# Two float32 layers behind a retention block: Strassen-like products against three-pass products of float32r parts, in two phases

## The chip, the core and the metric

The kernel runs on one core of a Trainium2 chip. The core has five engines with queues of their own: TensorE (PE in the profile, its weight loads PEld), VectorE (DVE), ScalarE (ACT), GpSimd (POOL) and SyncE (SP), which here only issues DMAs. They share an on-chip memory of 128 partitions, and TensorE writes its sums to eight PSUM banks of 512 float32 values per partition. The metric is the device time of one execution in microseconds; a version's time is the median of its runs.

## The reference

A retention block (a linear attention with a decaying state) over batch 4, 8 heads, 768 steps, head width 64, then two dense layers with an activation between them, over 4 x 768 = 3072 tokens:

```python
for t in range(S):
    state = gamma * state + np.einsum('bhd,bhe->bhde', k[:, :, t], v[:, :, t])
    y[:, :, t] = scale * np.einsum('bhd,bhde->bhe', q[:, :, t], state)
...
x = attn_out.transpose(0, 2, 1, 3).reshape(B * S, H * D)      # 3072 x 512
h = x @ w_in                                                   # w_in 512 x 2048
sp = np.maximum(h, 0.0) + np.log1p(np.exp(-np.abs(h)))         # softplus
g = h * erf(sp)
return (g @ w_out).astype(np.float32)                          # w_out 2048 x 512
```

q, k, v and the result are float32; w_in and w_out come as float64.

## The kernel before

The retention block works in 24 chunks of 128 steps. Chunks 0 to 3 take a longer way (`ret_scale`, `ret_transpose` on TensorE, `ret_scores`, `ret_mask`, `ret_out`). From chunk 4 on a chunk is handled as two halves of 64 steps: scores and state additions (`sub_begin`, or inside `sub_visit`), mask and new states on VectorE, results on TensorE, copies on ScalarE and two small sums on VectorE. Keys and queries from chunk 6 on are not transposed by TensorE: `load_blocks` fetches them in 32 x 32 blocks with 16 small DMAs for each of k and q (L187), and `prepared` scales them and transposes the blocks on VectorE. What comes out is x transposed (`xT`), the moving operand of the first layer.

The weights come as 64-bit words. `conversion` makes float32 of one piece (256 rows or columns, 1 MB) with five VectorE instructions and one of ScalarE. Its steps are handed out by `need` (until a block of weights is there) and `pace` (a budget of steps per matmul work). From the sixth piece on (in the changed kernel from the fifth to the seventh), `weights` puts the first step of the next piece between the third and fourth step of the present one.

The first 512 tokens go through both layers in plain float32 matmuls: `hidden_of` (L860) for the first layer, 512 columns at a time, `project` (L896) for the second. The rest runs in chunks of 256 tokens, each in two halves of the hidden width, so 20 groups `g`. Both layers then use bilinear schemes with fewer products: `hidden_steps` (L951) makes 26 products of blocks where 32 would be plain, from 18 sums of x (`X_SUMS`) and precomputed sums of the weights (`W_SUMS`), and adds or subtracts the products from PSUM into eight result blocks, on VectorE (L963) or ScalarE (L965, L967); `project_part` (L1034) makes 7 products where 8 would be plain, from sums of the gated values (`g_sums`) and of w_out. Between them `gate_softplus` (L817) and `gate_erf` (L830) on ScalarE and `gated` (L849) on VectorE. One group of the first layer runs in turn with products of the second layer of the group before it, so TensorE has work of one while VectorE and ScalarE finish the other. The first of these groups uses `hidden_plain` (L980) while sums of weights are still being made.

The order on every engine is the order in which the code is written (a manual schedule). All DMAs but two small ones and those for sums of w_out are issued by SP, in order; `load_block_scales` (L469, L473), with 17 tiny loads, stands at the third group. Outputs leave with `put_first` and `put_part`.

Of the kernel before, what the change touches and what calls it, by code (L numbers as in the profile page):

```python
# [12 lines left out]
F32 = mybir.dt.float32  # L13
U32 = mybir.dt.uint32
I64 = mybir.dt.int64
# [6 lines left out]
TCH = 512  # L22
FG = 4
SCH = 256
CV = 2


# [4 lines left out]

OUT = {"11": 0, "12": 1, "21": 2, "22": 3, "T3": 1, "T1": 4, "T2": 5, "T4": 6}

PRODUCTS = {
    1: ("11", "11"), 2: ("12", "21"), 3: ("S4", "22"), 4: ("22", "T4"),
    5: ("S1", "T1"), 6: ("S2", "T2"), 7: ("S3", "T3"),
}
# [6 lines left out]
N_W, N_X = 26, 18  # L45
W_SUMS = (
    (16, 2, 6, "+"),
    (17, 8, 10, "-"),
    (4, 4, 17, "+"),
    (10, 10, 16, "+"),  # L50
    (18, 16, 4, "-"),
    (19, 18, 5, "-"),
    (20, 1, 19, "-"),
    (20, 0, 20, "+"),
    (21, 9, 20, "+"),
    (9, 13, 9, "-"),
    (22, 15, 13, "-"),
    (23, 15, 9, "-"),
    (7, 3, 7, "+"),
    (24, 20, 12, "-"),  # L60
    (25, 18, 7, "+"),
    (2, 2, 3, "+"),
    (8, 12, 8, "-"),
    (12, 17, 12, "-"),
    (3, 3, 15, "-"),
    (15, 2, 15, "-"),
    (19, 19, 13, "-"),
    (16, 16, 7, "+"),
    (7, 7, 10, "+"),
    (4, 4, 6, "-"),  # L70
    (1, 1, 5, "+"),
    (5, 5, 2, "+"),
    (6, 14, 12, "+"),
    (6, 6, 15, "-"),
    (13, 23, 11, "-"),
    (13, 13, 7, "-"),
)

X_SUMS = (
    (0, (1, 0), (1, 1), "-"),  # L80
    (1, (0, 0), (0, 1), "-"),
    (2, (0, 0), (1, 0), "-"),
    (3, (1, 1), (0, 1), "-"),
    (4, (3, 0), (2, 0), "-"),
    (5, 1, 2, "-"),
    (6, (2, 0), 1, "+"),
    (7, (3, 1), 0, "-"),
    (8, (1, 1), (3, 1), "+"),
    (9, 6, (0, 1), "+"),
    (10, 7, 4, "-"),  # L90
    (11, (2, 0), 10, "-"),
    (12, (2, 1), 6, "-"),
    (13, (3, 1), 12, "-"),
    (14, 9, 13, "-"),
    (15, (3, 0), 13, "-"),
    (16, 15, 2, "+"),
    (17, 1, 15, "+"),
)

STEPS = (  # L100
    (21, (1, 0), 0, True, ((4, True),)),
    (20, 5, 1, True, ((1, False),)),
    (10, 14, 2, True, ((3, True),)),
    (22, 0, 3, True, ((5, True),)),
    (23, 7, 0, False, ((5, True),)),
    (24, (0, 1), 1, False, ((7, False),)),
    (25, 15, 2, False, ((2, True),)),
    (14, (2, 1), 3, False, ((7, True),)),
    (9, 8, 0, False, ((7, True),)),
    (12, 6, 1, False, ((6, False),)),  # L110
    (2, 11, 2, True, ((2, False), (6, True))),
    (17, 1, 3, True, ((2, False), (4, True))),
    (15, 10, 0, False, ((6, True),)),
    (8, 9, 1, False, ((4, False),)),
    (3, 4, 0, False, ()),
    (19, (1, 0), 0, False, ((0, True),)),
    (7, 13, 1, False, ((2, True),)),
    (0, 2, 2, False, ((0, True),)),
    (18, 16, 0, False, ((2, False),)),
    (16, 12, 1, False, ((3, True),)),  # L120
    (6, (2, 0), 3, False, ((6, True),)),
    (11, (3, 0), 2, True, ((4, True),)),
    (5, 0, 0, False, ()),
    (4, 17, 0, False, ((3, False),)),
    (1, 3, 0, False, ((1, True),)),
    (13, (3, 1), 1, False, ((5, False),)),
)

OP = {"+": ALU.add, "-": ALU.subtract}

BELOW = 1023 - 127
# [3 lines left out]
def kernel(  # L137
# [18 lines left out]
    NJ = B * NC  # L156
    n_k = d_model // P
    n_ft = d_ff // P
    JPC = TCH // C
    TT = TCH // P  # L160
    N = FG * TCH
    DH = d_model // 2
    assert D == 64 and d_model == H * D and n_k == HP == 4 and S % C == 0 and NJ % JPC == 0
    assert H == 8 and n_ft == 4 * FG and SCH == 2 * C and TCH == 2 * SCH

    const = ctx.enter_context(tc.tile_pool(name="const", bufs=1))
    loads = ctx.enter_context(tc.tile_pool(name="loads", bufs=3))
    ret = ctx.enter_context(tc.tile_pool(name="ret", bufs=2))
    act = ctx.enter_context(tc.tile_pool(name="act", bufs=2))
# [4 lines left out]


    early = True
    KQ, V, KB = {}, {}, {}

    NB = JPC + 2

    def load_blocks(to, src):


        for s, d in itertools.product(range(2), range(2)):
            part = slice((2 * s + d) * 32, (2 * s + d + 1) * 32)
            for u in range(HP):
                nc.sync.dma_start(  # L187
                    to[part, u * C : (u + 1) * C].rearrange("p (a d) -> p a d", d=32),
                    src[2 * u + s, :, d * 32 : (d + 1) * 32].rearrange("(a p) d -> p a d", p=32),
                )  # L190

    def load(j):
        b, c = divmod(j, NC)
        if j == JPC - 1:

            x = act.tile([P, N], F32, name="e", bufs=1)
            KQ[j] = x[:, : 2 * d_model].rearrange("p (i h d) -> p i h d", i=2, h=H)
            V[j] = x[:, 2 * d_model : 3 * d_model].rearrange("p (h d) -> p h d", h=H)
        else:
            KQ[j] = loads.tile([P, 2, H, D], F32, name="kq")  # L200
            V[j] = loads.tile([P, H, D], F32, name="v")
        now = slice(c * C, (c + 1) * C)
        if j >= NB:
            KB[j] = loads.tile([P, HP * C], F32, name="kb", bufs=2)
            nc.sync.dma_start(KQ[j][:, 0], k[b, :, now, :].rearrange("h p d -> p h d"))
            load_blocks(KQ[j][:, 1].rearrange("p h d -> p (h d)"), q[b, :, now, :])
            load_blocks(KB[j], k[b, :, now, :])
        for i, src in enumerate((k, q) if j < NB else ()):
            nc.sync.dma_start(KQ[j][:, i], src[b, :, now, :].rearrange("h p d -> p h d"))
        if not early:  # L210
            load_values(j)

    def load_values(j):
        b, c = divmod(j, NC)
        nc.sync.dma_start(V[j], v[b, :, c * C : (c + 1) * C, :].rearrange("h p d -> p h d"))
# [6 lines left out]
    w_in_sb = const.tile([P, 2, N_W, 2 * P], F32, name="w_in_sb")  # L222
    w_out_sb = const.tile([P, 2, 7, FG, DH], F32, name="w_out_sb")

    def w_in_of(ft, kk):
        half, s, i = ft // (2 * FG), ft % (2 * FG) // FG, ft % FG
        return w_in_sb[:, s, 4 * (2 * half + i // 2) + kk, i % 2 * P : (i % 2 + 1) * P]

    def w_out_of(ft):
        half, s, i = ft // (2 * FG), ft % (2 * FG) // FG, ft % FG  # L230
        return w_out_sb[:, s, 2 * half : 2 * half + 2, i, :]

    CE = 2 * d_model
    spare = [w_out_sb[:, s, 4:7].rearrange("p a b c -> p (a b c)") for s in range(2)]
    spare += [w_in_sb[:, s, 16:24].rearrange("p a f -> p (a f)") for s in (1, 0)]
    raws = [x[:, : 2 * CE].bitcast(I64) for x in spare]

    def halves(x):  # L240
        return x.rearrange("p (h c) -> p h c", h=2).bitcast(U32)

# [5 lines left out]
    for n in range(4):  # L248
        if n < 3:
            pieces += [("in", 2 * n + 2), ("in", 2 * n + 3)]  # L250
# [1099 lines left out]
```

## Time and profile before

| | us |
|---|---|
| runs (3), lowest / median / highest | 662.51 / 663.13 / 664.62 |
| span of the profiled execution | 660.9 |
| TensorE busy, weight loads busy | 655.7, 557.3 |
| VectorE, ScalarE, GpSimd busy | 508.4, 280.2, 11.7 |
| DMA | 51.88 MB, mean 78 GB/s |
| granted TensorE clock, mean | 1.000 |

The span runs from the first to the last instruction of the profiled execution. A row of the profile gives line, engine, operation, output and input tiles, shape and count, then the busy time and the mean of one in ns, then the idle time just before and what ended it. Matmuls are pipelined, so the mean of one is longer than the distance between two; the distance is read from the timeline, whose rows give start, length and a count of merged instructions. SPq rows are the DMA issues of SP's queue.

### The profile page before, as it was taken

Reading aid. Unit: us, or ns where it says so; the run is one execution under the profiler, and the core shown is the slowest. Engines: PE = TensorE matmul, PEld = TensorE weight load, DVE = VectorE, ACT = ScalarE, POOL = GpSimd, SP = SyncE. Lnnn points to the kernel's source line nnn. Section 1 sums busy time; section 2 is a strip of 40 time slices with the busy share of each in tenths; the row PEclk is TensorE's granted clock in tenths of the full one; section 3 lists DMA queues with packets and bytes.
Section 4 is the critical chain, followed back from the end, with each engine's and each line's share of the span. In section 5 each row is a group of like instructions: output and inputs, shape, how many; then the busy total and the mean of one; then the engine's idle time right before and its main releaser. Section 6 shows DMA issues by size and latency. Waiting matters only on the chain.

```text
span 660.9 us, 15247 instructions
## 1 busy us (share of the span) xinstructions
PE 655.7 (99%) x6200; PEld 557.3 (84%) x6200; DVE 508.4 (77%) x1102; ACT 280.2 (42%) x402; POOL 11.7 (2%) x29
## 2 busy tenths in 40 slices
PE   8999999999999999999999999999999999999998
PEld 7744444576999999999999999999999999999997
DVE  5999999969986786788678678677687688476464
ACT  3468363445534334244254253342432542533440
POOL 1000000110100000000000000000000000000000
PEclk9999999999999999999999999999999999999999
DMA  9999844385753321222222322221231210000000
GB/s 188 223 264 231 211 129 107 63 152 90 144 123 61 85 47 32 67 47 46 70 44 47 73 39 46 42 72 37 44 79 36 46 53 1 2 34 0 1 33 32
DMA packets 159413, 51.88 MB, mean 78 GB/s; under 512 B 143216, under 2 KB 149744, under 8 KB 159344
## 3 DMA queue, kind: packets, MB, share of 16 engines
q1 hardware_dynamic: 157776, 46.72, 32.8%
q0 software_dynamic: 1152, 4.19, 3.4%
q8 instruction: 48, 0.79, 0.5%
q14 instruction: 21, 0.17, 0.1%
q10 hardware_dynamic: 416, 0.01, 0.0%
HBM read 40.39 MB, written 6.29 MB: 71 GB/s over the span
## 4 chain that ended last, share of the span: by engine, by line
PE 98%; DMA 1%; DVE 0%; ACT 0%; issue 0%
PE o L1034 37%; PE hp L951 22%; PE r L951 12%; PE hp L860 8%; PE o L896 8%; PE hp L980 2%; PE r L736 2%; PE hp L628 1%; PE o L772 1%; PE r L524 1%; PE r L557 1%; PE o L604 1%; PE r L751 1%; PE hp L751 1%; DMA kq<-in_k_dram 1%; PE r L772 0%
## 5 line engine op out<-in xcount | busy, mean ns | idle before, releaser
L1034 PE MATMUL o<-w_out_sb,h 128*128 128x256 f32 (+1 forms) x640 | 142.7, 380 | 0.0
L951 PE MATMUL hp<-xs,w_in_sb 128*128 128x128 f32 x988 | 138.1, 275 | 0.0
L1034 PEld LDWEIGHTS o<-w_out_sb,h 128*128 128x128 f32 x640 | 119.5, 190 | 16.6
L963 DVE TENSOR_TENSOR h<-h,hp 128x256 f32<-128x256 f32 x190 | 78.0, 418 | 70.5 <-PE hp L951 65.6
L951 PEld LDWEIGHTS hp<-xs,w_in_sb 128*128 128x128 f32 x988 | 128.4, 192 | 3.0
L1034 PE MATMUL o<-w_out_sb,e 128*128 128x256 f32 x480 | 113.5, 379 | 0.0
L1034 PEld LDWEIGHTS o<-w_out_sb,e 128*128 128x128 f32 x480 | 86.8, 190 | 9.4
L817 ACT ACTIVATE e<-h 128x2048 f32<-128x2048 f32 x22 | 42.1, 1912 | 119.6 <-DVE h L963 119.6
L963 DVE TENSOR_TENSOR h<-h,r 128x256 f32<-128x256 f32 x152 | 56.9, 415 | 22.3 <-PE r L951 21.4
L965 ACT COPY h<-hp 128x256 f32<-128x256 f32 x38 | 14.2, 373 | 130.7 <-PE hp L951 122.7
L951 PE MATMUL r<-xs,w_in_sb 128*128 128x128 f32 x456 | 63.3, 275 | 0.0
L951 PEld LDWEIGHTS r<-xs,w_in_sb 128*128 128x128 f32 x456 | 57.0, 192 | 0.0
L860 PE MATMUL hp<-xT,w_in_sb 128*128 128x512 f32 (+2 forms) x144 | 56.5, 548 | 0.0
L849 DVE TENSOR_TENSOR e<-h,e 128x1024 f32<-128x1024 f32 x42 | 49.2, 1213 | 8.0 <-ACT e L830 8.0
L860 PEld LDWEIGHTS hp<-xT,w_in_sb 128*128 128x128 f32 x144 | 25.8, 190 | 27.0 <-issue 24.6
L951 PE MATMUL hp<-xT,w_in_sb 128*128 128x128 f32 x304 | 46.3, 275 | 0.0
L951 PEld LDWEIGHTS hp<-xT,w_in_sb 128*128 128x128 f32 x304 | 41.5, 192 | 1.4 <-issue 0.5
L830 ACT ACTIVATE e<-e 128x2048 f32<-128x2048 f32 (+1 forms) x23 | 42.1, 1836 | 0.2
L967 ACT ACTIVATE h<-hp 128x256 f32<-128x256 f32 x57 | 21.9, 384 | 29.7 <-PE hp L951 28.3
L951 PE MATMUL r<-xT,w_in_sb 128*128 128x128 f32 x228 | 31.7, 275 | 0.0
L830 ACT ACT_TABLE_LOAD x24 | 30.8, 1283 | 0.4
L951 PEld LDWEIGHTS r<-xT,w_in_sb 128*128 128x128 f32 x228 | 28.5, 192 | 0.0
(164 smaller groups left out, 799.0 us busy)
## 6 DMA issues: line engine op xcount, KB each, us to landing
w_out_sb<-in_moe_w_out_dram SPq DMA_DIRECT2D x14, 512.0 KB, 5.2
kq<-in_k_dram SPq DMA_DIRECT2D x23, 256.0 KB, 4.0
v<-in_v_dram SPq DMA_DIRECT2D x23, 256.0 KB, 3.4
out_dram<-r SPq DMA_DIRECT2D x23, 256.0 KB, 2.9
kq<-in_q_dram SPq DMA_DIRECT2D x288, 16.0 KB, 1.9
kb<-in_k_dram SPq DMA_DIRECT2D x288, 16.0 KB, 1.8
w_in_sb<-in_moe_w_in_dram SPq DMA_DIRECT2D x8, 512.0 KB, 10.1
w_out_sb<-w_out_sb POOLq DMA_DIRECT2D x8, 512.0 KB, 5.3
```

The source lines that it names most:

```text
L736: nc.tensor.matmul(pp[r][col * D : (col + 1) * D, u % 2, t], x[own, u, :], QT[j][own, u, t], start=first(r, col), stop=True, skip_group_ch ...
L751: nc.tensor.matmul(other[a][own, u % 2, D:] if crossed else pp[a][own, u % 2, t], V[j][t, 2 * u + r, :], AM[j][t, r, u, :D], start=crossed ...
L817: nc.scalar.activation(E[g], HS[g], AF.Softplus)
L830: nc.scalar.activation(E[g][:, half], E[g][:, half], AF.Erf)
L849: nc.vector.tensor_tensor(E[g][:, half], HS[g][:, half], E[g][:, half], op=ALU.mult)
L860: nc.tensor.matmul(HP_[ft][:, t], w_in_of(ft, kk), XC[0][:, kk, t], start=(kk == 0), stop=(kk == n_k - 1),)
L896: nc.tensor.matmul(O[0][tt].rearrange("p (d c) -> p d c", d=2), E[g][:, u * TCH + tt * P : u * TCH + (tt + 1) * P], w_out_of(ft), start=(f ...
L951: nc.tensor.matmul(to[:, u, :], w_in_sb[:, s, w, u * P : (u + 1) * P], XS[m](x), start=first and u == 0, stop=True, skip_group_check=True,)
L963: nc.vector.tensor_tensor(h, h, of, op=ALU.add if plus else ALU.subtract)
L965: nc.scalar.copy(h, of)
L967: nc.scalar.activation(h, of, AF.Copy, scale=-1.0)
L1034: nc.tensor.matmul(O[m][i][:, half, at], G[g][a][:, u * P : (u + 1) * P], w_out_sb[:, s, OUT[b], u, at], start=i not in started, stop=(s = ...
```

## The change

The file is written anew in most of its parts. Retention for chunks 0 to 5, the conversion of weights and the start are kept in substance. These differ:

- Both layers become plain products without Strassen-like sums. Each float32 factor is split into parts that a float32r operand holds exactly: `hi` (rounded by ScalarE as it writes float32r), `lo` (the rest) and `dif` (a combination of both). Three matmuls in float32r, of `hi`, `lo` and `dif`, into two PSUM sums, and `together` (one ScalarE and one VectorE instruction) combine to the full product.
- Phase one does retention and the first layer for all 3072 tokens, in groups of 256, each in 8 units of 256 hidden rows (`unit`). The sums h are stored to DRAM tiles `HID`, 25 MB in all. Groups 0 and 1 (the first 512 tokens) use plain float32 matmuls (`hidden_of`, 256 columns each), with stores in `put_hidden`.
- Phase two reads h back by halves of a group (`load_hidden`, 1 MB), gates it (`gate`, `gated`), splits it (`split_g`) and multiplies by w_out (`project`), 48 steps of 24 matmuls with 512 columns.
- w_out is converted during phase one, stored as float32 in DRAM (`WOF`) and read back and split at the end of phase one; the split of w_in is made around group 2.
- Keys and queries are loaded and prepared for two chunks at once (`load_pair`, `prepare`): 32 small DMAs and 4 larger ones per pair, five VectorE instructions of twice the width.
- `load_block_scales` moves to the first 128 hidden rows of the first 512 tokens.

The core of the diff (what the new functions replace is the code described above):

```diff
+Z = 2.0**-12
+KEEP = 1.0 - 2.0**-13
...
+    def split_weights(n, w=None):
+        w = WF.pop(n) if w is None else w
+        hi, lo, dif = (b4(f"w_{x}", [2 * d_model], F32R) for x in ("hi", "lo", "dif"))
...
+        nc.scalar.activation(hi, w, AF.Copy, scale=KEEP * Z)
+        nc.vector.scalar_tensor_tensor(lo, hi.bitcast(F32), -1 / Z, w, op0=ALU.mult, op1=ALU.add)
+        nc.vector.tensor_tensor(dif, hi.bitcast(F32), lo.bitcast(F32), op=ALU.subtract)
+        W[n] = hi, lo, dif
+
+    def split(to, at, x):
+        hi, lo, dif = (t[at] for t in to)
+        nc.scalar.activation(hi, x, AF.Copy, scale=KEEP)
+        nc.vector.tensor_tensor(lo, x, hi.bitcast(F32), op=ALU.subtract)
+        nc.vector.scalar_tensor_tensor(
+            dif, hi.bitcast(F32), Z, lo.bitcast(F32), op0=ALU.mult, op1=ALU.subtract
+        )
+
+    def together(to, a, b):
+        nc.scalar.activation(to, a, AF.Copy, scale=1 + 1 / Z)
+        nc.vector.scalar_tensor_tensor(to, b, -1 / Z, to, op0=ALU.mult, op1=ALU.add)
...
+    def load_pair(j):
...
+            for to, src in ((KB[j], k), (QB[j], q)):
+                for u in range(HP):
+                    nc.sync.dma_start(
+                        to[part, u].rearrange("p (a d) -> p a d", d=32),
+                        src[b, 2 * u + s, c * C : (c + 2) * C, d * 32 : (d + 1) * 32].rearrange(
+                            "(a p) d -> p a d", p=32
+                        ),
+                    )
+                yield
...
+    def unit(g, n):
+        if n in W:
+            own = next(turn)
+            a, b = (ps_o.tile([P, 2, GT], F32, name=f"o{2 * own + i}") for i in range(2))
+            for to, parts in ((a, (0, 1)), (b, (2,))):
+                for u in range(2):
+                    for kk, i in itertools.product(range(n_k), parts):
+                        nc.tensor.matmul(
+                            to[:, u],
+                            W[n][i][:, kk * 2 * P + u * P : kk * 2 * P + (u + 1) * P],
+                            X[g][i][:, kk],
...
+        def put():
+            h = b2("h", [2, GT])
...
+                together(h, a, b)
+            nc.sync.dma_start(HID[g][:, 2 * n : 2 * n + 2], h)
+        return put
...
+    during = {
+        0: [(load_block_scales,)],
+        1: [(K_, a)],
+        2: [(T, a, None, ("o2", "o3")), (steps, pair, 2)],
...
+        14: [(split_weights, 0)],
+        15: [(split_weights, 1)],
+    }
+    for ft in range(n_ft):
+        need("in", ft)
+        if ft:
+            hidden_of(ft, 0)
+        hidden_of(ft, 1)
...
+        need("in", min(ft + 2, n_ft - 1))
+        for f, *args in during.get(ft, ()):
+            f(*args)
+        put_hidden(ft)
...
+    def project(n):
...
+        for f, t in order:
+            ft = 4 * i + f
+            a, b = Y[g][t]
+            for x, to in enumerate((a, a, b)):
+                nc.tensor.matmul(
+                    to,
+                    G[n][x][:, f, t * P : (t + 1) * P],
+                    W[ft // 2][x][:, ft % 2 * d_model : (ft % 2 + 1) * d_model],
...
+    to_out = {
+        0: [(load_hidden, 0), (load_w_out, 0), (gate, 0)],
+        1: [(gated, 0), (load_hidden, 1), (load_w_out, 1), (split_w_out, 0)],
+        2: [(split_g, 0), (load_w_out, 2), (split_w_out, 1)],
+        3: [(split_g, 1), (load_w_out, 3), (split_w_out, 2)],
+        4: [(gate, 1), (load_w_out, 4), (split_w_out, 3)],
+        5: [(gated, 1), (load_hidden, 2), (load_w_out, 5), (split_w_out, 4)],
+        6: [(load_w_out, 6), (split_w_out, 5)],
+        7: [(load_w_out, 7), (split_w_out, 6)],
+    }
+    for g in range(G2, NG):
+        a, b = 2 * g + 2, 2 * g + 3
...
+        for n in range(NPC):
+            if more:
+                for f, j in {0: [(begin, a)], 2: [(results, a)], 3: [(begin, b)], 5: [(results, b)]}.get(n, ()):
+                    f(j)
+            put = unit(g, n)
+            steps(pair, 2)
+            if g == G2 and n < 4:
+                split_weights(n + 2)
+            if g == G2 + 1 and n in (1, 4):
+                split_weights(6 + n // 4)
+            if more:
+                if n == 0:
+                    states(a)
...
+                steps(prep, {5: 1, 6: 1, 7: 3}.get(n, 0))
+            if g > G2:
+                convert({1: 2, 2: 1, 4: 2}.get(n, 0) if a + 2 < NJ else 1)
+            put()
+            if g == NG - 1:
+                W.pop(n)
+                for f, *args in to_out[n]:
+                    f(*args)
+    split_w_out(NPC - 1)
+    for n in range(NG * NU):
+        g, i = divmod(n, NU)
+        project(n)
+        if n % 2 == 0:
+            split_g(n + 2)
+            if i == 0 and g:
+                for t in range(2):
+                    put_out(g - 1, t)
+            split_g(n + 3)
+            gate(n // 2 + 2)
+        else:
+            gated(n // 2 + 2)
+            load_hidden(n // 2 + 3)
```

## The prediction

> **What bounds the kernel now.** I read the page's busy lines and the chain of waits first, then TensorE's timeline for the true spacing of matmuls (a row's mean is a latency, since matmuls overlap), then the rows of the other engines and the DMA queue for prices.
>
> ```profile
> span 660.9 us, 15247 instructions
> PE 655.7 (99%) x6200; PEld 557.3 (84%) x6200; DVE 508.4 (77%) x1102; ACT 280.2 (42%) x402; POOL 11.7 (2%) x29
> ...
> PE 98%; DMA 1%; DVE 0%; ACT 0%; issue 0%
> ```
>
> TensorE alone sets the end, at full granted clock, so the change is worth what it does to TensorE's stream, plus any gap it opens in it. The timeline (start, length, name, count):
>
> ```profile
> 54.45 14.00 PE L896 MATMUL o<-w_out_sb,e 128*128 128x512 f32 x32
> 68.29 10.46 PE L860 MATMUL hp<-xT,w_in_sb 128*128 128x512 f32 x24
> ...
> 402.94 1.05 PE L951 MATMUL hp<-xs,w_in_sb 128*128 128x128 f32 x8
> 403.83 1.06 PE L951 MATMUL r<-xT,w_in_sb 128*128 128x128 f32 x8
> ...
> 408.33 0.46 PE L736 MATMUL r<-qT,state 64*64 64x64 f32 x16
> ...
> 410.35 7.17 PE L1034 MATMUL o<-w_out_sb,h 128*128 128x256 f32 x32
> 417.37 0.61 PE L951 MATMUL hp<-xT,w_in_sb 128*128 128x128 f32 x4
> ```
>
> From start to start: 13.84/32 = 432.5 ns at 512 columns, 7.02/32 = 219.4 at 256, 0.89/8 = 111.3 at 128: 0.83 ns a column and some 5 ns. One chunk's retention takes 410.35 - 408.33 = 2.02 us. The code writes 16 matmuls where 32 stand: an f32 matmul runs as two passes. Every pass has its own weight load:
>
> ```profile
> 402.72 1.08 PEld L951 LDWEIGHTS hp<-xs,w_in_sb 128*128 128x128 f32 x8
> 403.72 0.97 PEld L951 LDWEIGHTS r<-xT,w_in_sb 128*128 128x128 f32 x8
> ```
>
> Eight loads of 128 columns go by in the time of eight 111.3 ns passes, so a load every 111 ns stays hidden.
>
> ```profile
> L849 DVE TENSOR_TENSOR e<-h,e 128x1024 f32<-128x1024 f32 x42 | 49.2, 1213 | 8.0 <-ACT e L830 8.0
> L817 ACT ACTIVATE e<-h 128x2048 f32<-128x2048 f32 x22 | 42.1, 1912 | 119.6 <-DVE h L963 119.6
> L830 ACT ACT_TABLE_LOAD x24 | 30.8, 1283 | 0.4
> ...
> 410.08 8.66 SPq L187 DMA_DIRECT2D kq<-in_q_dram  x16
> ...
> 88.36 8.74 SPq L469 DMA_DIRECT2D kq_b<-decay_k_dram  x16
> ```
>
> Two L849 back to back take 2.36 us, so 1.15 us of VectorE each; likewise 0.6 at 512 and 0.34 at 256. A small load costs the SP queue 0.54 us of issue.
>
> **What TensorE loses and gains.** Gone: L951, 1976 passes x 111.3 = 219.9 us; L1034, 1112 x 219.4 + 16 x 111.3 = 245.8; L896, 128 x 432.5 = 55.4; L980, 64 x 219.4 = 14.0; together 535. New, by the built program: 1872 float32r matmuls of 256 columns, 1152 of 512, and 16 f32 matmuls of 256 (32 passes, 7.0).
>
> No row shows a float32r pass. Its price lies between half an f32 pass of its columns (111.3 and 219.4) and a whole one (219.4 and 432.5); I have no row under 0.83 ns a column, but the kernel gives a reason for the half: a float32 number is two parts of 12 bits (`Z`), a full product is four products of parts, the trace does it in two passes, hence two in a pass, and float32r operands here hold one part each. At half, a 256-column pass is like the 128-column f32 pass, load and all: 111.3. New sum 1872 x 0.1113 + 1152 x 0.2194 + 7.0 = 208.4 + 252.7 + 7.0 = 468. TensorE saves 67 us. At the whole price it loses 381.
>
> [...]
>
> **Where gaps open.** The rest is a walk through the built order, stage by stage.
>
> *First 512 tokens.* Until 27.3 us the order is the old one, less 1.0 for a first block of 256 instead of 384 columns: 26.3. Then 31 blocks of 8 passes x 219.4 = 54.4 and chunks 4 and 5 (two transposes of 1.0, four retention blocks of 1.1) 6.4: 87.1 without a gap. But the 17 loads of `load_block_scales` move from 88 us to the front of the SP queue, before the first store of sums and before w_in piece 4. Each DMA waits for the one eight before it, so they get past the eighth only when piece 3 has landed (8.9 MB at the 170 to 228 GB/s of the first four 10 us windows: 43 us); nine more x 0.54 = 48; piece 4 is issued at 49.6 and lands at 55; eight pair loads and piece 5 follow, landing at 64. `weights` puts the first step of piece 5 into piece 4's conversion, so VectorE stands there (and the states, sums and splits behind it) until 64, and piece 4 is ready at 67, where TensorE could use it at 57.5: 9.5 lost, 4 more on pieces 6 and 7. Stage: 100.
>
> *Groups 2 to 10.* A group is 8 units x 24 x 111.3 = 21.4, plus two chunks 4.0 = 25.4. VectorE has per group 8 `together` 4.8, masks and states 2.7, sums 0.8, splits of x 2.4, `prepare` 5.8, one weight piece 4.3 = 20.8: hidden in sum, not in place. Three steps of `prepare` (3.5 us) stand in unit 7 behind unit 6's `together` (0.85 after unit 6), and the next group's first matmuls need them: 0.85 + 2.3 against unit 7's 2.67, then the scaled keys 1.15 later, costs 1.5. SP needs 32 x 0.54 + 6.1 = 23.4 per group, starts behind the last store, and lands the key blocks about 1 us after VectorE asks: 0.95. So 27.9 per group in the eight groups 2 to 9. Group 2 has two f32 units (23.0 + 4.0) and four weight splits (1.5 lost), group 3 two splits (1.0): 28.5 + 8 x 25.4 + 8 x 2.45 + 1 = 252.3.
>
> *Group 11* is TensorE 21.4, but `to_out` puts the first gates and all w_out splits here. Sums of group 0 come back at 9.4 (issue at 3.9, 1 MB), gate 1.9 + 1.3 + 1.9 holds ScalarE to 14.5, and the `together` of unit 1 stands behind it, so unit 3 waits for its bank. From 15.1 VectorE is the bound, in its own order: seven `together` 4.2, `gated` twice 4.6, two splits of g 4.6 and six of w_out 13.8 = 27.2; unit 7's bank comes free at 42.3. First projection 42.4; 21 lost.
>
> *Projections.* 48 x 24 x 0.2194 = 252.7. Two of them (10.5) cover per gate: ScalarE two table loads 2.6, two functions 3.8, two splits 2.1, waits for `gated` 1.6, output copies 0.6 on average = 10.7 against 10.5, with 7 us in hand from the start, so hidden; if not, 0.2 x 24 = 5. VectorE 7.5. End: 4 (sum 0.7, store 2.9, like the end now).
>
> The stored sums (25 MB out, 25 back) I cost at nothing: a group moves 2.1 stored, 2.1 loaded for a pair, 1.6 for w_out = 5.8 MB in 27.9 us = 207 GB/s, where saturated early windows move up to 301; with 190 as the limit each group takes 30.5: 21 more.
>
> Sum 100 + 252.3 + 42.4 + 252.7 + 4 = 651.4 against this execution's 660.9. The runs' median is 2.2 above the span: 653 against 663. Runs spread over 0.3%, and less than that I call no change.
>
> **Rivals.**
> 1. No gaps of size: 87.1 + 231.7 + 21.4 + 252.7 + 4 = 597, run 599. For it: engines have room in sum. Against: the in-order queues above.
> 2. The SP queue sets the pace (slower). A pair load has 256 short rows, a row load before 128; if issue goes with rows, 1.08 us each, SP needs 40.7 per group, prepared keys come late, TensorE waits 12.8 x 8 = 103: run 756. It decides from 0.68 an issue, and from 0.72 the whole is slower than before. Against: the value loads of 1024 rows issue in 0.4.
> 3. A float32r pass costs a whole f32 pass, so the three passes do not do what they say: 651 + 1872 x 0.108 + 1152 x 0.213 = 1099, run 1101. No row excludes it.
> 4. DMA limit above: 672, run 674.
>
> **Chances.** Forecast 0.60 (its own range 632 to 675), rival 1 0.12, rival 2 0.13, rival 3 0.10, rival 4 0.05. Range 610 to 705: forecast and rival 4, the near half of rival 1, the near edge of rival 2. Faster: three quarters of the forecast plus rival 1, 0.57; same 0.07; slower 0.36.
>
> **What would show it.** Units 2.67 us and projections 5.27 from start to start (rival 3: twice). In the changed kernel's lines: a TensorE gap near 58 us released by DMA through VectorE; gaps of 1 to 3 us once a group before L492, released by VectorE's transposes; some 20 us lost in group 11, released by VectorE L259; none in the projections. Stores of 0.5 us on SP, pair loads at 0.54. I am wrong if the projections stand still for ScalarE, if group gaps exceed 5 us, or if a float32r load isn't hidden.

## The result, and the profile after

The changed kernel takes 715.6 us (median of four runs, 714.1 to 717.5), the kernel before 662.9 (four runs beside them, 662.5 to 664.6): a ratio of 1.080, 95% interval 1.077 to 1.082. The forecast was 653, with 610 to 705 as its range. The change is slower, and by 10 us more than the range allowed.

The head of the page of after, TensorE's two rows of slices, and the chain of waits:

```profile
span 712.4 us, 14414 instructions
PE 645.6 (91%) x6072; PEld 574.4 (81%) x6072; DVE 485.6 (68%) x625; ACT 340.1 (48%) x384; POOL 7.6 (1%) x20
...
PE   8993699999979898798999675999999999999997
PEclk9997799999989999989999978899999999999999
...
PE 36%; DMA 3%; DVE 1%; issue 1%; SPq 0%; ACT 0%; DVEq 0%
```

TensorE was busy 99% of the span and set 98% of the chain; now it is busy 91%, and the chain could be followed back only to 412 us, through the last part. The row of slices shows three places where it is short of work (slices 4 and 5, dents from slice 12 to 19, slices 23 to 25), and the clock row dips with it. So time was lost in gaps, and beside the gaps at a lower clock (0.959 on average). The ledger by the prediction's stages, each boundary read off TensorE's timeline:

| stage | forecast, us | measured, us | difference |
|---|---|---|---|
| first 512 tokens (to 111.35) | 100 | 111.35 | +11.3 |
| groups 2 to 10 (to 395.3) | 252.3 | 283.9 | +31.6 |
| group 11 (to 437.0) | 42.4 | 41.7 | -0.7 |
| projections (to 708.1) | 252.7 | 271.1 | +18.4 |
| end | 4 | 4.3 | +0.3 |
| span | 651.4 | 712.4 | +61.0 |

First the price of a pass. TensorE's timeline of after: start, length, name, count. Lengths overlap; the starts are what counts.

```profile
114.03 0.28 PE L608 MATMUL o<-x_hi,w_hi 128*128 128x256 f32 x1
114.15 0.28 PE L608 MATMUL o<-x_lo,w_lo 128*128 128x256 f32 x1
...
560.29 0.39 PE L786 MATMUL r<-w_dif,g_dif 128*128 128x512 f32 x1
560.51 0.39 PE L786 MATMUL hp<-w_hi,g_hi 128*128 128x512 f32 x1
```

From start to start, 0.12 us at 256 columns and 0.227 at 512 (24 passes of a projection take 5.44). Half of an f32 pass, as assumed, but not quite: 120 for 111.3 and 226.7 for 219.4. The prices of VectorE and ScalarE held, as the costliest groups show (mean ns of one behind the busy time; 1213 and 1912 before):

```profile
L747 DVE TENSOR_TENSOR e<-hid,e 128x1024 f32<-128x1024 f32 x48 | 56.6, 1221 | 56.4 <-ACT e L739 56.4
...
L738 ACT ACTIVATE e<-hid 128x2048 f32<-128x2048 f32 x24 | 46.1, 1920 | 7.3 <-DMA hid<-hid 7.1
```

The same matmuls behind a group's gap:

```profile
203.04 0.69 PE L492 MATMUL hp<-qT,kT 64*64 64x64 f32 x32 [3.52 <-DVE qT L472]
204.25 1.14 PE L499 MATMUL hp<-v,kn 64*64 64x64 f32 x32 [0.52 <-DVE kn L476]
...
205.69 0.41 PE L608 MATMUL o<-x_lo,w_lo 128*128 128x256 f32 x1
205.91 0.41 PE L608 MATMUL o<-x_hi,w_hi 128*128 128x256 f32 x1
```

TensorE waited 3.52 and 0.52 us, and its next 256-column passes stand 0.213 us apart instead of 0.12: the granted clock is 0.50 from 203.8 to 210.6 us. Four of the gaps do this (before 203, 236, 301 and 336 us); the one of 1.86 us before 269 does not.

The gap in the first 512 tokens, TensorE's row first and then SyncE's queue (start, length and name of what it issued) in the order of time:

```profile
74.47 8.65 PE L586 MATMUL hp<-xT,w 128*128 128x256 f32 x32 [14.99 <-DVE w L200]
```
```profile
38.43 10.73 SPq L329 DMA_DIRECT2D kq_b<-decay_k_dram  x16
49.20 1.46 SPq L333 DMA_DIRECT2D by_b<-decay_s_dram  x1
...
51.71 1.27 SPq L152 DMA_DIRECT2D raw<-in_moe_w_in_dram  x2
...
57.43 4.46 SPq L122 DMA_DIRECT2D qb<-in_q_dram  x4
...
62.97 1.26 SPq L152 DMA_DIRECT2D raw<-in_moe_w_in_dram  x2
```

The two rows at L152 are w_in pieces 4 and 5: one is issued behind the 17 block scales, the other behind the first pair loads. VectorE's rows name the rest:

```profile
59.86 0.69 DVE L181 TENSOR_SCALAR power<-raw 128x1024 uint32<-128x1024 uint32 x1 [7.75 <-DMA raw<-in_moe_w_in_dram]
...
61.19 1.23 DVE L189 SCALAR_TENSOR_TENSOR w<-w,raw 128x1024 f32<-128x1024 uint32 x1
71.23 0.69 DVE L181 TENSOR_SCALAR power<-raw 128x1024 uint32<-128x1024 uint32 x1 [8.82 <-DMA raw<-in_moe_w_in_dram]
```

In the middle of piece 4 it stands 8.8 us for the landing of piece 5. This is the place that the prediction named, with 15.0 us lost where it had 9.5. Behind the gap the clock is down here too: the 32 passes at 74.47 take 8.65 us, where a block later in the stage takes 7.14; the granted clock is 0.50 from 74.4 to 77.5 us.

A group, on SyncE, and VectorE's wait in it:

```profile
172.76 3.79 SPq L122 DMA_DIRECT2D kb<-in_k_dram  x4
...
190.67 3.31 SPq L122 DMA_DIRECT2D kb<-in_k_dram  x4
...
201.46 3.68 SPq L631 DMA_DIRECT2D hid<-h  x4
205.19 3.49 SPq L122 DMA_DIRECT2D kb<-in_k_dram  x4
```
```profile
195.82 1.23 DVE L466 TENSOR_TENSOR kb<-kb,kq_b 128x1024 f32<-128x1024 f32 x1 [3.91 <-DMA kb<-in_k_dram]
```

SyncE begins a group's pair loads when the last store of the group before is out (172.76, then 205.19). It goes through the rows by fours, stores between them, and issues the last key block of the pair at 190.67 to 193.98; VectorE has waited 3.91 us for it. VectorE's scaling, transposes and last addition follow, then the next last store. That is a loop of 32.4 us: 21.2 of SyncE to the last key block, 1.8 to its landing, and 9.4 through VectorE's work to the store behind it. Groups 4 to 7 take 32.6 to 33.0 us each, start to start. The 32 loads of a pair take 20.6 us of SyncE, 0.64 each, not 0.54. Most of them go by in 0.5 us; the average is raised by a few long ones, four of which wait for the landing of the DMA eight before (2.6 us together).

The phase switch, on ScalarE in group 11:

```profile
406.37 1.91 ACT L738 ACTIVATE e<-hid 128x2048 f32<-128x2048 f32 x1 [7.08 <-DMA hid<-hid]
...
420.49 1.06 ACT L242 ACTIVATE w_hi<-w 128x1024 fp32r<-128x1024 f32 x1 [5.50 <-DMA w<-wof]
421.45 0.58 ACT L258 ACTIVATE h<-o 128x512 f32<-128x512 f32 x1
...
442.29 1.06 ACT L242 ACTIVATE w_hi<-w 128x1024 fp32r<-128x1024 f32 x1 [6.67 <-DMA w<-wof]
```

The addition of a unit (L258) stands behind a split (L242) that waits for its piece of w_out, 5.50 and 6.67 us here. SyncE issues that piece only behind the store of an earlier unit, and that store waits for that unit's addition: a loop through a DMA, not VectorE's work. The first row is the gate, which waits 7.08 us for the sums of group 0.

### The profile page after: what moved, and what is told of

Its sections match the earlier page's. It is cut to its first block, busy times and chain, and to the rows that moved or that the text cites. A ratio compares the mean times of both kernels' runs of the same rounds, so it can differ in the third digit from the quotient of the medians.

```text
span 712.4 us, 14414 instructions
## 1 busy us (share of the span) xinstructions
PE 645.6 (91%) x6072; PEld 574.4 (81%) x6072; DVE 485.6 (68%) x625; ACT 340.1 (48%) x384; POOL 7.6 (1%) x20
## 5 line engine op out<-in xcount | busy, mean ns | idle before, releaser
L608 PE MATMUL o<-x_hi,w_hi 128*128 128x256 f32 x624 | 165.9, 301 | 11.8 <-ACT h L258 11.8
L608 PE MATMUL o<-x_lo,w_lo 128*128 128x256 f32 x624 | 161.2, 293 | 0.0
L608 PEld LDWEIGHTS o<-x_hi,w_hi 128*128 128x128 f32 x624 | 126.4, 203 | 15.0 <-ACT h L258 12.4
L608 PEld LDWEIGHTS o<-x_lo,w_lo 128*128 128x128 f32 x624 | 126.6, 203 | 0.0
L258 ACT ACTIVATE h<-o 128x512 f32<-128x512 f32 x78 | 46.3, 593 | 159.5 <-PE o L608 136.2
L608 PE MATMUL o<-x_dif,w_dif 128*128 128x256 f32 x624 | 89.1, 286 | 1.5 <-DVE h L259 1.5
L608 PEld LDWEIGHTS o<-x_dif,w_dif 128*128 128x128 f32 x624 | 82.2, 196 | 1.7 <-DVE h L259 1.7
L786 PE MATMUL o<-w_dif,g_dif 128*128 128x512 f32 x192 | 75.6, 394 | 4.3 <-DVE h L259 4.3
L586 PE MATMUL hp<-xT,w 128*128 128x256 f32 x256 | 61.0, 397 | 20.1 <-DVE w L200 18.4
L786 PE MATMUL o<-w_hi,g_hi 128*128 128x512 f32 x192 | 75.6, 394 | 2.9 <-ACT h L258 2.9
L786 PE MATMUL o<-w_lo,g_lo 128*128 128x512 f32 x192 | 75.5, 393 | 0.0
L250 ACT ACTIVATE g_hi<-e 128x1024 fp32r<-128x1024 f32 x48 | 50.8, 1060 | 30.4 <-DVE e L747 29.1
```

The lines of the kernel that those rows point to most:

```text
L250: nc.scalar.activation(hi, x, AF.Copy, scale=KEEP)
L258: nc.scalar.activation(to, a, AF.Copy, scale=1 + 1 / Z)
L586: nc.tensor.matmul(HP_[ft][:, g], w[:, kk, ft % 2 * P : (ft % 2 + 1) * P], XC[g][:, kk], start=(kk == 0), stop=(kk == n_k - 1),)
L608: nc.tensor.matmul(to[:, u], W[n][i][:, kk * 2 * P + u * P : kk * 2 * P + (u + 1) * P], X[g][i][:, kk], start=(u == 0 and kk == 0 and i == ...
L786: nc.tensor.matmul(to, G[n][x][:, f, t * P : (t + 1) * P], W[ft // 2][x][:, ft % 2 * d_model : (ft % 2 + 1) * d_model], start=ft == 0 and ...
```

## The experiments

All times of single runs are beside a run of the kernel before at 662.6 to 662.8 on the same chip; a run lies 1.6 to 1.8 us above its span. The four runs of after lie 3.4 us apart, so smaller differences between single runs are read from the stages and not from the total.

**The price of a pass.** A kernel that leaves the whole computation out and only runs streams, 48 float32r matmuls or 24 f32 ones (two passes each) of one form, weights loaded before each one:

```
...
for cols in (512, 384, 256, 192, 128, 64):
    f32r(48, cols)
f32r(48, 256, 64); f32r(48, 256, 32); f32r(48, 128, 64)   # 64, 32 weight columns
...
for _ in range(6):
    small(16); f32r(16, 256)                               # 64x64 f32, then float32r
```

> This kernel leaves the whole computation out and only runs streams of matmuls on one chunk of k. Theory A: a matmul instruction costs its columns (0.417 ns each in float32r, 0.833 ns in f32 twice over) and a fixed 12 to 13 ns, paid once per instruction whatever its passes: float32r 512, 384, 256, 192, 128, 64 columns at 227, 173, 120, 93, 66, 39 ns; f32 of 128 columns at 222 ns. Theory B: the load of 128 weight columns sets a floor of 107 to 120 ns: float32r of 192, 128 and 64 columns all stay at 110 to 120 ns, and 256 columns with only 64 or 32 weight columns go faster than 120. Switching between 64x64 f32 matmuls and full float32r ones: if it has a price of its own, a block of 16 small and 16 large takes about 0.2 us more than 16 x 32 + 16 x 120 ns; if not, nothing more.

Measured, as the distance of the first matmuls of two streams in the timeline by 48 (ns; TensorE at full clock; the 64-column stream and the one of 256 columns with 64 weight columns, where it was not, are left out):

```
float32r, 128 weight columns:  512: 229   384: 174   256: 120   192: 111.5   128: 111.0
float32r, 256 columns, 32 weight columns: 113     128 columns, 64 weight columns: 60
f32,      128 weight columns:  256: 2 x 216 to 218       128: 2 x 110
```

The floor of theory B is there: from 192 columns down the load of 128 weight columns holds a float32r pass at 111 ns, and with half the weight columns 128 columns take 60. Theory A has the form right above it: from 256 columns up a float32r pass costs 0.42 to 0.43 ns a column and 10 to 13 more. Part of this constant belongs to the weights, since 256 columns with 32 weight columns take 113. The other part of theory A, the same constant once for both passes of an f32 matmul, does not come out: at the 0.83 ns a column of f32 an f32 matmul of 256 columns keeps 5 to 9 ns, not 12 to 13, so 3 to 5 a pass. The row of 111.3 that the prediction took as the price could not show this. For an f32 pass of 128 columns the columns (106 ns, an estimate: 128 x 0.83) and the floor (111) nearly coincide, so it tells neither how much of it is constant nor where the floor begins. At half of 0.83 ns a column a float32r pass of 256 columns has 106 ns of columns too, and 13 beside them (an estimate from the 119.6 ns between two).

The blocks of the same kernel, small and large matmuls in turn:

```profile
115.44 1.15 PE L93 MATMUL o<-x 64*64 64x64 f32 x32
116.52 2.18 PE L88 MATMUL o<-xr,ws 128*128 128x256 f32 x16
118.62 1.15 PE L93 MATMUL o<-x 64*64 64x64 f32 x32
```

Sixteen float32r passes take 2.10 us (116.52 to 118.62) where 16 x 119.6 = 1.91 were due: 0.19 more. With eight f32 matmuls in their place (two passes each), 3.66 for 16 x 0.218 = 3.49, so it is not float32r's own. The small block pays as well: its 32 passes take 1.08 us, where an unbroken stream of them at the end of this kernel has 29.2 ns each, 0.93 for 32. A small block between large ones so costs some 0.33 us beside its own work (an estimate: 0.19 and 1.08 - 0.93).

**Block scales off SyncE.**

```
-                nc.sync.dma_start(          # load_block_scales, 16 + 1 loads
+                nc.gpsimd.dma_start(
```

> Only change: the 17 loads of the block scales are issued from the GpSimd queue instead of SyncE's. Theory (the loads stand ahead of w_in piece 4 on SyncE): the 15.0 us gap near 59 us falls below 5, the first 512 tokens end at 99 to 102 us instead of 111.3, run 702 to 706. Rival (w_in simply cannot come faster through the DMA engines in the first 60 us): the gap stays over 10 us, run 711 or more.

709.7. The gap falls to 6.6 us and the first 512 tokens end at 105.2: the direction of the theory and some half of its size; all three of its numbers are missed. Piece 4 is now issued at 40.96 instead of 51.71, but piece 5 still stands behind eight pair loads, at 55.41, and TensorE's gap ends 11.5 us after that issue, as it does in after (62.97 and 74.47).

**No interleave.**

```
-        for n, steps in enumerate(pending):        # weights()
...
-                if 4 <= n < NPC - 1 and k == 2:
-                    next(pending[n + 1])
...
+        for n in range(2 * NPC):
+            for _ in conversion(n):
+                yield
```

> Only change: the first step of w_in piece n+1 no longer stands inside the conversion of piece n. Theory (piece 4 has long landed while VectorE stands at piece 5): TensorE gets piece 4 some 10 us earlier, the 15.0 us gap splits into two of 3 to 5 us, the first 512 tokens end 5 to 9 us before 111.3, run 706 to 711. Rival (the landing of the pieces sets the pace, the interleave only chooses where the wait is seen): the first 512 tokens end within 2 us of 111.3, run 713 to 717.

711.8, with the first 512 tokens at 111.7. TensorE's rows:

```profile
65.53 8.74 PE L580 MATMUL hp<-xT,w 128*128 128x256 f32 x32 [6.25 <-DVE w L200]
...
90.57 9.86 PE L580 MATMUL hp<-xT,w 128*128 128x256 f32 x32 [6.56 <-DVE by_b L330]
102.91 2.47 PE L580 MATMUL hp<-xT,w 128*128 128x256 f32 x5 [2.49 <-DVE w L200]
```

One gap of 15 and one of 3 have become four of 6.3, 1.5, 6.6 and 2.5: the rival is right for this stage, though the run lies between its number and the theory's. The pieces' issue in SyncE's queue sets the pace, and the interleave only chooses where the wait is seen. (The single run is 3.8 us under the median of after and 2.3 under its fastest; that comes from later groups, whose periods differ by some us from run to run.)

**Query blocks off SyncE.**

```
-            for to, src in ((KB[j], k), (QB[j], q)):
+            for to, src, queue in ((KB[j], k, nc.sync), (QB[j], q, nc.gpsimd)):
                 for u in range(HP):
-                    nc.sync.dma_start(
+                    queue.dma_start(
```

> Only change: the 16 query loads of a pair are issued from the GpSimd queue, SyncE keeps the 16 key loads, the values, the stores and the w_out pieces. Theory (SyncE's issue from the last store of a group to the last key block sets the period, 32.6 us in the middle groups): periods fall to 28.5 to 30.5 us, run 690 to 702. Rival (VectorE's three preparing steps in unit 7 set it): periods stay above 31.5 us, run 708 or more. If GpSimd needs over 1.5 us to issue one of these loads, the query blocks come late instead and the run is slower than 716.

694.0, the theory. Groups 3 to 10 start 29.1 to 29.3 us apart, all of them: the loop through SyncE was what set their period. Busy time by stretch (length, then PE, PEld, DVE, ACT, POOL, the granted clock, DMA share, GB/s), of after and of this kernel:

```profile
200.00:230.00 30.00, 26.44 (x396) 25.59 (x397) 19.25 (x32) 6.85 (x13) 0.00 (x0) 0.89 0.67 170
```
```profile
200.00:230.00 30.00, 29.15 (x447) 28.13 (x440) 22.88 (x37) 8.04 (x15) 8.75 (x16) 1.00 0.75 195
```

With the waits gone the clock is back, 1.00 over the whole of 200 to 350 us where after had 0.93, and the DMA engines move more, not less. What SyncE waits for has changed with it, in after and here:

```profile
SPq L631 <- DVE h L259: 80.8, 27, 12.2
```
```profile
SPq L631 <- DVE h L259: 144.9, 58, 12.0
```

Of the 80 stores of these groups SyncE came early enough to wait for 27; now it does for 58. GpSimd issues a query block in 0.58 us. VectorE's three steps in unit 7, to which the prediction gave 1.5 us per group, cost TensorE 0.43 and 0.41 us (0.90 and 0.41 in group 4).

**Warm matmuls in the group gaps.**

```
+        for _ in range(warm):               # begin(a), 8 in groups 3 to 10
+            nc.tensor.matmul(SC[j][0][:, 0, :], ident, ident, start=True, stop=True)
```

> As the changed kernel, with eight matmuls of 128 columns that nobody reads (8 x 0.22 = 1.8 us) ahead of the first block of each of groups 3 to 10, where TensorE waits for the transposed blocks. Theory (the passes at 0.21 us behind those waits are the lower granted clock, and the idle time brings it): the granted clock of the stretch 200 to 370 us goes from 0.89 to 0.94 up to 0.97 or more, no passes of 0.21 us behind most group starts, run 706 to 712. Rival (the slow passes come with their operands, not with the idle time): clock as before, run 716 to 722.

721.6, the rival's number, and the clock from 200 to 370 us is 0.95 (0.94 in after), the rival's too. But it is no clean test of the idle time, since the waits did not go. The gaps did not shrink by the 1.8 us put into them; in three groups 2.3 us of waiting are left behind the eight matmuls:

```profile
239.75 1.13 PE L494 MATMUL hp<-qT,kT 64*64 64x64 f32 x32 [2.34 <-DVE qT L472]
```
```profile
200.00:230.00 30.00, 27.53 (x429) 26.54 (x429) 20.02 (x32) 7.45 (x14) 0.00 (x0) 1.00 0.68 178
230.00:260.00 30.00, 26.76 (x359) 25.66 (x358) 19.74 (x30) 5.79 (x10) 0.00 (x0) 0.89 0.73 183
```

Where the rest of the wait is short (1.21 us, before 205 us) the clock stays at 1.00, where it was 0.89; where 2.34 us are left it falls again. That speaks for the idle time as the cause of the low clock, as the run with the query blocks moved does more plainly. The eight matmuls cost more than they saved; why the groups became longer by 0.9 us each on average was not followed up.

**w_out loaded early.** Sums 0 and two pieces in group 10, the others two units ahead:

```
+    early = {4: [(load_hidden, 0)], 5: [(load_w_out, 0)], 6: [(load_w_out, 1)]}
...
-        3: [(split_g, 1), (load_w_out, 3), (split_w_out, 2)],
+        3: [(split_g, 1), (load_w_out, 5), (split_w_out, 2)],
```

> Only change: in group 10 already the sums 0 and the first two pieces of w_out are loaded, and in group 11 each other piece two units ahead of its split instead of one. Theory (the chain store of sums, load of a piece, ScalarE's split, next addition sets group 11): the first projection starts at 424 to 431 us instead of 437.0 and the gaps behind it go, run 698 to 706. Rival (VectorE's own work in group 11, as the prediction had it): the first projection starts at 433 or later, run 710 or more.

700.8, the first projection at 426.1: the theory, but for the gaps behind that start, of which two stay (2.34 and 2.03 us). VectorE's rows now:

```profile
412.31 1.22 DVE L243 SCALAR_TENSOR_TENSOR w_lo<-w_hi,w 128x1024 fp32r<-128x1024 f32 x1
413.56 1.22 DVE L244 TENSOR_TENSOR w_dif<-w_hi,w_lo 128x1024 fp32r<-128x1024 f32 x1
414.70 0.68 DVE L259 SCALAR_TENSOR_TENSOR h<-o,h 128x512 f32<-128x512 f32 x1
```

No row of it waits from 404 to 444 us. The limit that the prediction gave to group 11, VectorE, is there once the DMA loop is gone, and not before.

**w_out's splits spread.** Two of them in group 10, one behind the first projection (with a dict of their own, since w_in's parts are still in use):

```
+        4: [(split_w_out, 0)], ... 6: [(split_w_out, 1)]      # early, group 10
...
+        if n == 0:
+            split_w_out(NPC - 1)                             # behind project(0)
```

> As the kernel with w_out loaded early, and the splits of w_out's first two pieces moved into group 10 and that of the last one behind the first projection, so 7.4 us of VectorE's work leaves group 11. Theory (with the loads early VectorE is what bounds group 11, 1.23 us for each half of a split): the first projection starts at 417 to 421 us instead of 426.1, run 691 to 697. Rival (ScalarE's gate of 6.4 us and its order set it): first projection at 424 or later, run 699 or more.

694.2, inside the theory's range for the run, but the first projection starts at 424.5, the rival's number. What was won lies behind it: the waits for banks in the first projections, 2.34 and 2.03 us with the early loads alone, are down to one of 2.03. From the start of group 10 to the second projection it is 66.1 us instead of 73.8: 7.7 won, for 7.4 us of VectorE's work moved away. That fits VectorE as the bound of the phase switch as a whole, though the loads moved earlier as well. It does not bound the start of the first projection; whether ScalarE's gate does is argued here, not shown.

**The edits together**: the first three that gained; then with no interleave and spread splits.

> The three edits together: scales and query blocks from the GpSimd queue, w_out early. If each closes a gap of its own, they add: 715.6 - 5.9 - 21.6 - 14.8 = 673, so 669 to 677. If the two on the GpSimd queue get in each other's way, or the phase switch's gap only moves, 682 or more.

672.5. They add to within a microsecond of 673.

> Scales and query blocks from the GpSimd queue, no interleave, w_out early and its splits spread. Theory (the kernel's loss is in gaps; the float32r stream itself is shorter than the old one): floor from the trace is 87 us for the first 512 tokens, 9 x 29.2 for the groups, 23 for group 11, 48 x 5.44 for the projections and 4.2 for the end, 638 and 640 with what lies around the span; with 8 to 20 us of gaps left the run is 650 to 664, at or below the kernel before. Rival (TensorE's clock or the DMA engines take back what the gaps give): 672 or more.

661.6, as the theory had it; beside the 662.6 of the kernel before, one run each, that is no difference. The first 512 tokens end at 98.6 us, where the three edits had 102.6: without the interleave, which was worth nothing alone, 4 us are gained once the queue in front of it is clear.

**A version to beat both.** First more splits in group 10 and an earlier load of chunk 4, then retention in three places of a group instead of four:

```
+        6: [(split_w_out, 1)], 7: [(split_w_out, 2)],         # early
...
+    load(JPC)                                                # ahead of load_piece(2, 0, 1)
...
-    {0: [(begin, a)], 2: [(results, a)], 3: [(begin, b)], 5: [(results, b)]}
+    {0: [(begin, a)], 3: [(results, a), (begin, b)], 5: [(results, b)]}    # the second kernel
```

> As the kernel with all gaps closed, and three of w_out's splits in group 10 instead of two, the last two behind the first two projections, and chunk 4's keys and queries loaded ahead of w_in piece 2. If VectorE's work is what still holds group 11 (waits of 2.25 and 2.03 us) and the late keys what holds TensorE at 42 us (3.87 us), these go: run 652 to 657. If ScalarE's gate or the bytes of the first 40 us set them, 659 or more.

660.3, short of the 652 to 657 hoped for: the phase switch gains 3 us as meant (group 10 to the first projection 56.8 instead of 58.1, the rest in the projections), but the first stage gives 2 back. TensorE waits 2.2 us less for the keys, and the pieces behind them come later (new waits of 1.2 and 2.8 us on VectorE).

> As c3, with a chunk's results put beside the next chunk's first block, so that retention stands in three places of a group instead of four. If each change between retention's small matmuls and float32r passes costs 0.2 to 0.3 us, a group takes 28.9 to 29.0 instead of 29.2 to 29.3 and the run is 2 to 3 us under c3's. If it costs nothing, the same as c3; if the states come late by this order, slower.

661.3. A group takes 28.96 us instead of 29.29, so one small block between float32r units less is worth 0.33, as the streams had it; but a wait of 2.2 us opens where group 3 hands over to group 4, group 2 ends 2.4 us later than in the version before (waits of 1.83 and 1.11 us at its start, and passes 0.21 us apart behind them), and the run is no better.

> As c3 with the load order of the first 40 us as it was, results beside the next chunk's first block only in groups 3 to 10, and each of the first two gates in two parts a unit apart, so that ScalarE is away for 3.2 us at a time instead of 6.4. From the spans: all-gaps kernel 659.9, less 3 for the phase switch as c3 has it, less 8 x 0.33 for the retention blocks, less 1 to 3 for the parted gates: span 651 to 654, run 653 to 656 against 662.7 before, ratio 0.985 to 0.990. If the parted gates or the mixed orders open new waits, 659 or more, no different from before.

656.2 (four runs, 655.5 to 657.0) against 663.1 (seven runs): a ratio of 0.990, interval 0.988 to 0.991. The span is 0.8 above the expected range: the parted gates gain 1.3 us (group 10 to the first projection 55.5 instead of 56.8), but the hand-over from group 3 still costs 2.2.

```profile
span 654.8 us, 14516 instructions
PE 629.2 (96%) x6072; PEld 561.8 (86%) x6072; DVE 484.0 (74%) x625; ACT 339.9 (52%) x384; POOL 98.8 (15%) x181
...
PEclk9979999998999999999999989999999999999999
```

The same matmuls as in after, TensorE busy 96% of the span instead of 91%, and 57.6 us shorter. It beats the kernel before by 1%.

The hand-over wait is the same in this kernel and in the one before it. Here, behind 2.24 and 0.41 us, the passes are 0.21 us apart; there (second rows), behind the same two waits, 0.12:

```profile
159.05 0.69 PE L486 MATMUL hp<-qT,kT 64*64 64x64 f32 x32 [2.24 <-DVE qT L466]
...
161.60 0.41 PE L602 MATMUL o<-x_lo,w_lo 128*128 128x256 f32 x1
161.81 0.41 PE L602 MATMUL o<-x_hi,w_hi 128*128 128x256 f32 x1
```
```profile
163.10 0.69 PE L487 MATMUL hp<-qT,kT 64*64 64x64 f32 x32 [2.24 <-DVE qT L467]
...
165.06 0.28 PE L603 MATMUL o<-x_lo,w_lo 128*128 128x256 f32 x1
```

So behind 2.24 and 0.41 us the passes stood at half rate in one run and at full rate in the other: the length of a wait alone does not decide.

## Why the prediction was wrong, step by step

No rival alone is what happened. The run is the forecast's own sum with terms that were too small, and one, the clock, that was not in it; the step that failed first is the price of a float32r pass.

**Right: the half price, in kind.** Rival 3 is out: a unit is 2.88 us and a projection 5.44, not twice the forecast. The runs show the price alone; that it is half because a pass makes two products of parts was the author's inference from `Z` and the two passes of an f32 matmul.

**Wrong in size: "At half, a 256-column pass is like the 128-column f32 pass, load and all: 111.3".** It is 120, and 226.7 for 219.4. Over 78 units of 24 passes that is 16.3 us, over 1152 passes of the projections 8.4: 24.7 in all. TensorE's saving on products shrinks with it from 67 us to 42. The rows that were halved are f32 rows, which carry 5 to 6 ns beside the columns of a pass; a float32r pass carries 13 (at half of 0.83 ns a column), and the row of 128 columns lies where columns and floor nearly coincide (106 and 111 ns) and could not show it.

**Wrong in size: retention at 2.02 us a chunk.** That number came from an order in which all blocks of a chunk stand in one place. In the new order a group's retention stands in four places between float32r units, and the run with the query loads moved shows 29.2 - 8 x 2.88 = 6.2 us per group, some 0.9 of it small waits, so 5.3 for two chunks instead of 4.0: some 12 us over nine groups. Two small blocks more per group at 0.33 us each are 0.7 of the 1.3 (an estimate from the streams and from the kernel with three places); the rest was not followed up.

**Missing: the clock.** Full speed was assumed throughout; the mean granted clock is 0.959. A group with a gap before it takes 1.5 to 2.5 us longer for its first three units even without the gap, in four groups: 8.0 us together. The trace of after shows half-rate passes behind waits of 3.52 + 0.52, 3.71 + 1.16, 2.28 + 0.41 and 1.48 + 1.10 us, though not behind 1.86 + 0.41; behind 2.24 + 0.41 one of the two last kernels shows them and the other does not. So no length of wait can be given here from which they must come; but the sum needed a price for the clock beside its gaps of over 2 us, at least as a chance.

**The group gaps: right in sum, for a reason only half seen.** The waits at group starts come to 19.3 us, 22 forecast. But the forecast split them into 1.5 of VectorE's order and 0.95 of SyncE's lateness, and without the query loads on SyncE both parts go together. The step that was right was "SP needs ... per group, starts behind the last store"; its size was off, 0.64 us an issue for 0.54, and the loop was not closed: behind SyncE's last key block come 1.8 us to the landing and 9.4 of VectorE's work before the last store lets SyncE go on. Even at 0.54 that is 29.2 us (an estimate, 32.4 less 32 x 0.10), over the 27.9 of the forecast. That is rival 2's mechanism at a price just below the 0.68 from which it was to decide. It was not an alternative to the forecast; it was the larger part of it.

**The first 512 tokens: right in place, short by 11.3.** Block scales ahead of piece 4 and piece 5's first step inside piece 4 are both in the trace. The 16 scales took 0.67 us each instead of 0.54, and the eight pair loads ahead of piece 5 took 7.7 us (54.15 to 61.89). TensorE's waits in the stage come to 19.1 us for 13.5 forecast, and some 3.2 are the clock again: the blocks behind the gaps of 15.0 and 3.0 us take 8.65 and 8.83 us, not 7.14.

**Group 11: 41.7 for 42.4, and by another cause.** VectorE was to be the bound. It was busy 38.4 of the 56 us from 406 to 462; the loop of store, load, split and addition held it. With the loads early the first projection comes 11 us sooner, and then VectorE is busy without a pause, with the prices that were forecast. A right number was no sign of a right reason here.

**Projections: 271.1 for 252.7.** 8.4 of it is the price of a pass; 10 lie in the first of them, which starts at 437.0, waits 2.84, 2.92 and 1.42 us for banks that the late additions still hold, and runs at half clock (0.51 from 442.7 to 449.6 us). ScalarE and VectorE stay hidden behind the others, as forecast. Rival 4 fell too: the DMA engines moved 195 GB/s over 30 us of the groups once SyncE let them, over the 190 that it took as a limit.

Together: 23.0 for passes (the 1.7 of group 11 are in its own line), 12 for retention, 8 for the clock in groups, 11.3 for the first stage, 10 for the start of the projections, 0.3 for the end, less 2.9 for gaps forecast and not there, less 0.7: 61.0, as measured. That the terms, rounded one by one, meet it so well is in part luck. It is an account of TensorE's time, not of what each cause is worth alone: in groups 4 to 7 SyncE's loop set the period, and there cheaper passes would have met longer waits. The largest single term is the pass; without it and with the rest as measured the run would still have been slower than before.

## What to carry to other kernels

A price per pass must be split into columns, a constant per instruction, and the floor of the weight load before it is halved (for float32r here 0.42 to 0.43 ns a column, 10 to 13 ns, and 111 ns with 128 weight columns). A row where columns and floor nearly coincide, as 106 and 111 ns do here, cannot tell the parts from each other. When products get cheaper, the slack of every in-order queue shrinks with them: ask which queue (here SyncE with 0.64 us per small load, waits included, in a loop with VectorE and the last store) now takes longer than the matmuls of a stage, and look for loops through a DMA, not only for sums of busy time. Put a clock loss beside each gap of TensorE that lasts some us: here 0.50 for 6.8 us behind waits of 3.52 and 0.52 us, and nothing behind 1.86 and 0.41.

## What the runs showed of the hardware

The granted clock can fall without a pause. In the kernel of streams, TensorE has no gap, yet behind 64-column passes (27 ns of columns each, an estimate at 0.42 ns a column; 44 passes in the 5.00 us of the second row) it drops to 0.50:

```profile
72.00:76.00 4.00, 4.00 (x38) 4.00 (x38) 0.00 (x0) 0.00 (x0) 0.00 (x0) 1.00 0.00 0
77.00:82.00 5.00, 5.00 (x44) 5.00 (x44) 0.00 (x0) 0.00 (x0) 0.00 (x0) 0.94 0.00 0
82.90:88.00 5.10, 5.10 (x25) 5.10 (x26) 0.00 (x0) 0.00 (x0) 0.00 (x0) 0.50 0.00 0
```

The first row is the stream of 128 columns (54 ns in each 111, by the same estimate), at full clock; the second is the stream of 64 columns, and the third follows it. So TensorE can be busy all the time in the profile's sense and still get half the clock, 5.10 us of 5.10 at 0.50 in the third row. What brings the drop is not shown; it was seen behind one stream, and it stays an observation.
